# Order changes in a window-attention and ReGLU kernel: heating and bias of unit 1, chain of unit 2, transposes of batch 2, and the end in three pieces

## The chip, the cores and the metric

The kernel runs on one core of one Trainium2 chip. The metric is the device time of one execution in microseconds. Each kernel is timed in several executions, and one execution carries a trace. A page of the profile gives the *span* (first to last instruction); the device time is about 1.7 us longer than the span. The engines are PE (TensorE, the matmuls; PEld is its weight loads), DVE (VectorE), ACT (ScalarE) and POOL (GpSimd); PSUM is the memory in which matmul results land. The *granted clock* is the share of PE's full clock that it was given. Ratios are the mean time of one kernel's fast runs (all within 1.5% of its fastest) over that of the kernel before in the same rounds, so they are not quite the ratios of the medians quoted.

## The reference, cut to what matters

```python
# q, k, v: (8, 8, 576, 64); attention over a causal window of 64 tokens
scores = scale * np.matmul(q, k.transpose(0, 1, 3, 2))
mask = (rel >= 0) & (rel < 64)
attn = softmax(np.where(mask, scores, -1e9))
attn_out = np.matmul(attn, v)
# then a gated feed-forward net on all 4608 tokens of 512 features
x = attn_out.transpose(0, 2, 1, 3).reshape(4608, 512)
out = (np.maximum(x @ w_gate, 0) * (x @ w_val)) @ w_out      # 1536 hidden features
```

## The kernel before

Attention runs in 24 *units* of 192 tokens of one sequence (three units to a batch), the feed-forward net in 12 *tiles* of 384 tokens, two units to a tile. A hand-written scheduler, the weaver, interleaves them: each piece of work is queued with a planned time, and while the feed-forward matmuls are emitted, whatever is due is emitted between them. A planned time fixes only the order of instructions on each engine. Hidden features are made in 12 blocks `f`; a hidden tile of the text is one PSUM tile `h` (gate or value side), and a *gate* is the DVE product `g_sb` of both sides.

One unit needs: scores (`st`, PE), exponentials (`p`, ACT), masks (DVE), values (`pv`, PE), then copies of the values out of PSUM (`xv`, ACT), transposes of the sums (`sT`, DVE), reciprocal, spreading (`rs`) and multiply (`xt`, DVE). Units 0 and 1 use a bias matmul in place of the mask. q and k of each batch pass through DVE transposes first (`qT`, `kT`, about 1.25 us each, four to a batch).

```python
def heat(n, to, start=True):            # matmuls on zeros, to keep PE busy
    for _ in range(n):
        nc.tensor.matmul(to, zero[:, 0:128], zero[:, 0:to.shape[1]], ...)

def plan_unit(u, T, exp=0.8, mask=1.5, pv=3.9, copy=(4.7, 6.0),
              norm=(4.8, 6.1, 7.4, 8.7), gap=0.6):
    W.at(T, lambda: u_st(u))
    for g in range(G):
        W.at(T + exp + gap * g, lambda g=g: u_exp(u, g))
        W.at(T + mask + gap * g, lambda g=g: u_mask(u, g))
    ...                                 # copies at copy, values at pv
    # norm: two halves of the sums' transposes, reciprocal + spreading, multiply

W.at(5.4, lambda: heat(10, units[0]["spare"], False))
W.at(8.7, lambda: u_st(0, (0,)))
W.at(9.5, lambda: heat(8, units[0]["spare"], False))
W.at(11.0, lambda: u_st(0, (1,)))
...                                     # cut: exponentials and copies
W.at(11.4, lambda: u_pv(0, (0, 1)))
W.at(11.45, lambda: u_bias(1, (2, 3)))  # half of unit 1's bias
W.at(11.5, lambda: u_pv(0, (2, 3)))
W.at(11.6, lambda: u_bias(1, (0, 1)))
W.at(11.7, lambda: u_st(1))
...                                     # cut
plan_unit(2, 24.0, *fast)
...
for t in range(3, NU // 2):             # T grows by 26.525 a tile
    for u, at, tr in ((2 * t, T + 0.5, early), (2 * t + 1, T + 13.2, late)):
        if u == 2 * UB:
            plan_batch(2, 36.9, (50.0, T + 0.3, T + 1.7, T + 3.1))
        ...
    plan_unit(2 * t, T + (5.0 if t == 3 else 0.5))
    plan_unit(2 * t + 1, T + 13.2, ...)
```

The softmax here doesn't subtract the row's maximum and nothing guards it: scores larger than these inputs give would overflow.

Of the kernel before, what the change touches and what calls it, by code (L numbers as in the profile page):

```python
# [9 lines left out]
FP32 = mybir.dt.float32  # L10
# [32 lines left out]
def kernel(  # L43
# [10 lines left out]
    nc = tc.nc  # L54
    B, H, S, D = q.shape
    DM = H * D
# [9 lines left out]
    TT = 2 * U  # L66
# [10 lines left out]
    f_sb = ctx.enter_context(tc.tile_pool(name="f_sb", bufs=3))  # L77
# [5 lines left out]
    wo = persist.tile([128, NF, DM], FP16)  # L83
# [44 lines left out]
    W = Weaver()  # L128
    units = {}
# [32 lines left out]
    def qk_load(b, name, hh):  # L162

        tile_ = nat[b, name, hh] = a_in.tile([128, S // 32 * D], FP16, name=f"{name}{hh}", bufs=2)
        src = (q if name == "q" else k)[b, G * hh:G * hh + G]
        nc.gpsimd.dma_start(tile_, src.rearrange("h (i j) d -> (h i) (j d)", i=32))
# [31 lines left out]
    def u_bias(u, gs=range(G)):  # L198

        d = units.setdefault(u, {})  # L200
        if "st" not in d:
            st_tiles(u)
        d["biased"] = True
        for to in d["st"][0] + d["st"][1] if u == 0 else [d["st"][0][g] for g in gs]:
            n = to.shape[1] // 256
            nc.tensor.matmul(to.rearrange("p (h c) -> p h c", h=n), ident,  # L206
                             bias.rearrange("p w c -> p (w c)")[:, None, :].to_broadcast([128, n, 256]),
                             start=True, stop=False, skip_group_check=True)

    def heat(n, to, start=True):  # L210

        for _ in range(n):
            nc.tensor.matmul(to, zero[:, 0:128], zero[:, 0:to.shape[1]], start=start, stop=start, skip_group_check=not start)
# [140 lines left out]
    def plan_batch(b, load, trans):  # L354
        for i, (name, hh) in enumerate((n, hh) for n in "kq" for hh in range(2)):
            if load is not None:
                W.at(load, lambda name=name, hh=hh: qk_load(b, name, hh))
            W.at(trans[i], lambda name=name, hh=hh: qk_trans(b, name, hh))
# [90 lines left out]
    def output_last(t):  # L449

        last = TT // 128 - 1
        output(t, range(last))
        W.drain()
        for col in range(2):
            op = op_tile()
            for f in range(NF):
                g_sb, _ = gs[t]
                nc.tensor.matmul(op[:, 0:256], g_sb[:, f, bass.ds(last * 128, 128)], wo[:, f, 256 * col:256 * col + 256],  # L458
                                 start=(f == 0), stop=(f == NF - 1))
            parts = ((0, 256, nc.scalar.copy, nc.sync),) if col == 0 else (  # L460
                (0, 128, nc.scalar.copy, nc.scalar), (128, 256, nc.vector.tensor_copy, nc.sync))
            o_sb = f_sb.tile([128, DM], FP32, name="o_sb")
            for c0, c1, copy, queue in parts:
                copy(o_sb[:, c0:c1], op[:, c0:c1])
                queue.dma_start(out[bass.ds(t * TT + last * 128, 128), 256 * col + c0:256 * col + c1], o_sb[:, c0:c1])

    def output_by_rows(t):
        ops = [op_tile() for _ in range(TT // 128)]
# [8 lines left out]
    with tc.manual_schedule():  # L477
        for hh in range(2):
            k_first(hh)
        for hh in range(2):  # L480
            qk_load(0, "q", hh)
        warm = consts.tile([128, 2], FP32)
        nc.vector.memset(warm, 0.0)
        nc.scalar.activation(warm[:, 1:2], warm[:, 0:1], ACT.Exp)
        zero = consts.tile([128, 512], FP16)
        nc.vector.memset(zero, 0.0)
        st_tiles(0)
        heat(12, units[0]["st"][1][3])
        bands()
        constants()  # L490
        v_ones(1, nc.vector)
        for hh in range(2):
            for part in range(2):
                k_round(hh, part, 2)
        W.at(5.0, lambda: qk_trans(0, "k", 0, 0, 9))
        W.at(5.1, band_bias)
        W.at(5.2, lambda: qk_trans(0, "k", 0, 9, 18))
        W.at(7.0, lambda: qk_trans(0, "q", 0))
        W.at(8.6, lambda: qk_trans(0, "k", 1, 0, 9))
        W.at(8.7, lambda: qk_trans(0, "k", 1, 9, 18))  # L500
        W.at(9.9, lambda: qk_trans(0, "q", 1))
        G3, V3, O3 = ([(wt, src, f0, f0 + 4) for f0 in (0, 4, 8)]
                      for wt, src in ((wg, moe_w_gate), (wv, moe_w_val), (wo, moe_w_out)))
        W.at(5.5, lambda: v_load(0))
        W.at(5.6, lambda: v_load(1))
        W.at(6.4, lambda: w_load(*G3[0], 13.7))
        W.at(6.5, lambda: w_load(*V3[0], 16.3))
        W.at(6.6, lambda: w_load(*G3[1], 18.9))
        W.at(9.9, lambda: w_load(*V3[1], 21.5))
        W.at(9.9, lambda: w_load(*G3[2], 24.1))  # L510
        W.at(9.9, lambda: w_load(*V3[2], 26.7))
        W.at(12.3, lambda: v_load(2))
        W.at(12.6, lambda: w_load(*O3[0], 31.2))
        W.at(12.7, lambda: w_load(*O3[1], 33.8))
        W.at(12.8, lambda: w_load(*O3[2], 36.4))
        plan_batch(1, None, (37.5, 39.0, 40.4, 41.8))
        W.at(13.0, lambda: qk_load(1, "k", 0))
        W.at(13.0, lambda: qk_load(1, "k", 1))
        W.at(13.0, lambda: qk_load(1, "q", 0))
        W.at(13.0, lambda: qk_load(1, "q", 1))  # L520
        W.at(13.1, lambda: v_load(3))
        W.at(30.0, lambda: v_load(4))
        W.at(30.1, lambda: v_load(5))
        W.at(5.3, lambda: u_bias(0))
        W.at(5.4, lambda: heat(10, units[0]["spare"], False))
        W.at(8.7, lambda: u_st(0, (0,)))
        W.at(9.5, lambda: heat(8, units[0]["spare"], False))
        W.at(11.0, lambda: u_st(0, (1,)))
        for g in range(G):
            W.at(9.6 + 0.05 * g, lambda g=g: u_exp(0, g, 0))  # L530
            W.at(11.1 + 0.05 * g, lambda g=g: u_exp(0, g, 1))
            W.at(12.0 + 0.05 * g, lambda g=g: u_copy(0, g))
            W.at(12.3 + 0.05 * g, lambda g=g: u_exp(1, g))
        W.at(11.4, lambda: u_pv(0, (0, 1)))
        W.at(11.45, lambda: u_bias(1, (2, 3)))
        W.at(11.5, lambda: u_pv(0, (2, 3)))
        W.at(11.6, lambda: u_bias(1, (0, 1)))
        W.at(11.7, lambda: u_st(1))
        W.at(11.9, lambda: u_sum(0, 0))
        W.at(12.0, lambda: v_before(1))  # L540
        W.at(12.1, lambda: u_sum(0, 1))
        W.at(12.2, lambda: u_back(0))
        W.at(12.5, lambda: u_norm(0))
        W.at(12.6, lambda: u_pv(1))
        W.at(12.7, lambda: u_sum(1, 0))
        W.at(12.8, lambda: u_sum(1, 1))
        for n in range(4):
            W.at(12.9, lambda n=n: u_copy(1, n))
        W.at(13.2, lambda: u_back(1))
        W.at(13.3, lambda: u_norm(1))  # L550
        W.at(21.0, lambda: v_ones(2, nc.vector))
        W.at(18.0, lambda: v_before(2))
        W.at(21.0, lambda: v_ones(0, nc.vector))
        W.at(22.0, k_zeros)
        fast = 0.8, 1.5, 3.9, (4.1, 5.3), (4.2, 5.4, 6.4, 7.5), 0.5
        plan_unit(2, 24.0, *fast)
        plan_unit(3, 42.5, *fast)
        plan_unit(4, 50.0)
        plan_unit(5, 58.0, *fast)
        T = 68.4  # L560
        early, late = (-7.4, -6.0, -4.6, -3.2), (-20.3, -18.9, -17.5, -16.1)
        for t in range(3, NU // 2):
            for u, at, tr in ((2 * t, T + 0.5, early), (2 * t + 1, T + 13.2, late)):
                if u == 2 * UB:
                    plan_batch(2, 36.9, (50.0, T + 0.3, T + 1.7, T + 3.1))
                elif u % UB == 0:
                    plan_batch(u // UB, at + tr[0] - 10, [at + x for x in tr])
            plan_unit(2 * t, T + (5.0 if t == 3 else 0.5))
            plan_unit(2 * t + 1, T + 13.2, copy=(4.7, 5.8), norm=(4.8, 5.9, 6.9, 8.0))
            T += 26.525  # L570
        W.advance(13.7)
        ready(1)
        hidden(0, 0, U, 0, 4, 4)
        ready(2)
        hidden(0, U, TT, 0, 4, 4)
        hidden(0, 0, TT, 4, NF, 4)
        output_by_rows(0)
        ready(3)
        hidden(1, 0, U)
        output(1, (0,))  # L580
        ready(4)
        hidden(1, U, TT)
        output(1, (1, 2))
        for t in range(2, NU // 2):
            ready(2 * t + 2)
            hidden(t, 0, TT)
            (output if t < NU // 2 - 1 else output_last)(t)
        W.drain()
# [30 lines left out]
```

## Time and profile before

| | kernel before |
|---|---|
| timed executions | 342.64 to 342.87 us (median 342.76, 3 runs) |
| the traced execution | 344.84 us, span 343.1, mean granted TensorE clock 0.995 |
| busy share PE / DVE / ACT | 97% / 73% / 54% |

Views of the trace are shown in the prediction. In a timeline line, the numbers are start and length in us; the bracket is the engine's idle time before the instruction and what ended it. In a line of windows, the numbers are the window and its length, then busy us of PE, PEld, DVE, ACT, POOL, then granted clock, DMA share and GB/s. The 16 pairs of L305 that the prediction times are a weight load and a 128-column value matmul each.

### The profile page before, as it was taken

Reading aid. Unit: us, or ns where it says so; the run is one execution under the profiler, and the core shown is the slowest. Engines: PE = TensorE matmul, PEld = TensorE weight load, DVE = VectorE, ACT = ScalarE, POOL = GpSimd, SP = SyncE. Lnnn points to the kernel's source line nnn. Section 1 sums busy time; section 2 is a strip of 40 time slices with the busy share of each in tenths; the row PEclk is TensorE's granted clock in tenths of the full one; section 3 lists DMA queues with packets and bytes.
Section 4 is the critical chain, followed back from the end, with each engine's and each line's share of the span. In section 5 each row is a group of like instructions: output and inputs, shape, how many; then the busy total and the mean of one; then the engine's idle time right before and its main releaser. Section 6 shows DMA issues by size and latency. Waiting matters only on the chain.

```text
span 343.1 us, 7364 instructions
## 1 busy us (share of the span) xinstructions
PE 332.7 (97%) x2950; PEld 201.2 (59%) x2950; DVE 251.5 (73%) x452; ACT 186.7 (54%) x383; POOL 65.7 (19%) x99
## 2 busy tenths in 40 slices
PE   8789999999999999999999999999999999999996
PEld 4476477956646556555555655654664664664653
DVE  5587948998898775797888873878968974875430
ACT  4547157645737546556565565564664663763322
POOL 8723421420122211220120410420120200000000
PEclk9899999999999999999999999999999999999999
DMA  8999998790361941961352962874306401001002
GB/s 214 176 206 196 201 167 150 87 178 31 25 84 42 166 58 63 158 74 63 23 48 77 116 80 92 89 100 105 25 5 119 33 2 71 22 2 62 31 2 93
DMA packets 59666, 30.29 MB, mean 88 GB/s; under 512 B 46064, under 2 KB 51056, under 8 KB 59632
## 3 DMA queue, kind: packets, MB, share of 16 engines
q0 software_dynamic: 53872, 19.21, 52.4%
q1 hardware_dynamic: 5616, 10.55, 8.3%
q8 instruction: 23, 0.38, 0.4%
q14 instruction: 11, 0.09, 0.1%
q10 hardware_dynamic: 144, 0.07, 0.1%
HBM read 39.58 MB, written 9.44 MB: 143 GB/s over the span
## 4 chain that ended last, share of the span: by engine, by line
PE 80%; DVE 11%; issue 4%; DMA 2%; POOL 1%; ACT 1%; ACTq 0%; DVEq 0%; POOLq 0%
PE h L412 48%; PE op L426 21%; PE pv L305 6%; DVE sT L335 3%; PE st L246 3%; DVE g_sb L400 2%; DMA v<-in_v_dram 2%; DVE qT L184 2%; DVE xt L350 1%; DVE rs L344 1%; DVE p L266 1%; DVE kT L184 1%; PE op L458 1%; PE pv L287 1%; PE st L206 1%
## 5 line engine op out<-in xcount | busy, mean ns | idle before, releaser
L400 DVE TENSOR_TENSOR g_sb<-r_sb,h 128x384 f16<-128x384 f32 x144 | 78.3, 549 | 54.0 <-PE h L412 45.8
L412 PE MATMUL h<-xt,wg 128*128 128x384 f16 (+1 forms) x640 | 116.5, 310 | 0.7 <-DVE xt L350 0.7
L412 PE MATMUL h<-xt,wv 128*128 128x384 f16 (+1 forms) x640 | 116.6, 310 | 0.2 <-ACT r_sb L397 0.2
L397 ACT ACTIVATE r_sb<-h 128x384 f32<-128x384 f32 x144 | 71.2, 496 | 51.3 <-PE h L412 43.1
L426 PE MATMUL op<-wo,g_sb 128*128 128x512 f16 x420 | 93.3, 379 | 0.5 <-DVE g_sb L400 0.5
L412 PEld LDWEIGHTS <-wg 128*128 128x128 f16 x640 | 59.3, 98 | 34.7 <-DVE xt L350 1.4
L412 PEld LDWEIGHTS <-wv 128*128 128x128 f16 x640 | 59.7, 98 | 32.0 <-issue 0.5
L192 POOL DMA_DIRECT2D v<-in_v_dram x48 | 40.4, 846 | 189.5 <-PE pv L305 170.1
L426 PEld LDWEIGHTS <-g_sb 128*128 128x128 f16 x420 | 40.9, 98 | 48.8 <-issue 1.1
L335 DVE STREAM_TRANSPOSE sT<-pv 64x384 f32<-64x384 f32 x88 | 51.1, 580 | 11.4 <-PE pv L305 9.8
L260 ACT ACTIVATE p<-st 128x512 f16<-128x512 f32 x92 | 49.9, 604 | 11.6 <-PE st L246 11.4
L433 ACT COPY o_sb<-op 128x512 f32<-128x512 f32 x35 | 20.5, 586 | 61.1 <-PE op L426 61.0
L323 ACT COPY xv<-pv 64x384 f32<-64x384 f32 x88 | 41.7, 474 | 18.3 <-DVE sT L335 8.5
L266 DVE TENSOR_TENSOR p<-p,mask 128x512 f16<-128x512 f16 x88 | 34.2, 420 | 6.5 <-ACT p L260 5.9
L305 PE MATMUL pv<-p,v 128*128 128x128 f16 x352 | 24.1, 219 | 0.4 <-DVE p L266 0.4
L344 DVE STREAM_TRANSPOSE rs<-rT 128x768 f32<-128x768 f32 x24 | 23.5, 979 | 0.8
L305 PEld LDWEIGHTS <-v 128*128 128x128 f16 x352 | 21.6, 98 | 3.7 <-issue 0.9
L350 DVE TENSOR_TENSOR xt<-xv,rs 128x768 f16<-128x768 f32 x24 | 22.7, 947 | 0.7
L184 DVE STREAM_TRANSPOSE kT<-k 128x576 f32<-128x576 f32 (+1 forms) x18 | 19.8, 1119 | 1.9 <-ACT k L177 1.8
L184 DVE STREAM_TRANSPOSE qT<-q 128x576 f32<-128x576 f32 x16 | 19.0, 1239 | 0.9 <-DMA q<-in_q_dram 0.8
L246 PE MATMUL st<-qT,kT 32*128 32x128 f16 x768 | 16.1, 215 | 2.2 <-DVE qT L184 2.2
L246 PEld LDWEIGHTS <-kT 32*128 32x128 f16 x768 | 11.5, 92 | 10.5 <-issue 10.5
(46 smaller groups left out, 80.3 us busy)
## 6 DMA issues: line engine op xcount, KB each, us to landing
out_dram<-o_sb SPq DMA_DIRECT2D x35, 256.0 KB, 2.0
v<-in_v_dram POOLq DMA_DIRECT2D x38, 128.0 KB, 4.0
q<-in_q_dram POOLq DMA_DIRECT2D x16, 288.0 KB, 8.3
k<-in_k_dram POOLq DMA_DIRECT2D x14, 288.0 KB, 6.4
wg<-in_moe_w_gate_dram POOLq DMA_DIRECT2D x3, 512.0 KB, 11.2
wv<-in_moe_w_val_dram POOLq DMA_DIRECT2D x3, 512.0 KB, 13.0
wo<-in_moe_w_out_dram POOLq DMA_DIRECT2D x3, 512.0 KB, 16.3
k<-in_k_dram SPq DMA_DIRECT2D x2, 576.0 KB, 4.0
```

Source lines behind the costliest of these rows:

```text
L184: nc.vector.transpose(dst.rearrange("p (i j) -> p j i", i=32)[:, j0:j1], src[:, j0:j1])
L192: nc.gpsimd.dma_start(v16[p0:128, w, :, 0:64], v[b, :, k0 + p0:k0 + 128].rearrange("h p d -> p h d"))
L246: nc.tensor.matmul(d["st"][hh][g][:, c:c + 128], kT[rows, hh, ks + 128 * w:ks + 128 * w + 128, dh], qT[rows, hh, ks + 64 * w:ks + 64 * w + ...
L260: nc.scalar.activation(d["p"][g].rearrange("p h c -> p (h c)"), d["st"][0][g], ACT.Exp, scale=scale)
L266: nc.vector.tensor_tensor(p, p, mask.rearrange("p w c -> p (w c)")[:, None, :].to_broadcast([128, 2, 256]), MUL)
L305: nc.tensor.matmul(d["pv"][c % 2][:, c // 2, e, 64 * w:64 * w + 128], v16[:, w, 128 * h - 64 * e:128 * h - 64 * e + 128], d["p"][h % G][:, ...
L323: nc.scalar.copy(d["xs"][rows, n::2], d["pv"][n][rows, :, e, 0:U])
L335: nc.vector.transpose(to[64 * e:64 * e + 64, half::2], d["pv"][half][64 - 64 * e:128 - 64 * e, :, e, 0:U])
L397: nc.scalar.activation(part(r_sb), part(h1), ACT.Relu)
L400: nc.vector.tensor_tensor(g_sb[:, f:f + w, c0:c1], part(r_sb), part(h2), MUL)
L412: nc.tensor.matmul(h[:, b * n:b * n + n], wt[:, c, (f + b) * 128:(f + b) * 128 + 128], xt[:, c, c0:c1], start=(c == 0), stop=(c == NC - 1))
L426: nc.tensor.matmul(op, g_sb[:, f, bass.ds(sub * 128, 128)], wo[:, f], start=(f == 0), stop=(f == NF - 1))
```

## The change

Four parts. *Start:* more heating, and half of unit 1's bias ahead of unit 0's values, where PE waited. *Unit 2:* its normalising goes behind all gates of tile 0, into tile 0's output matmuls, and batch 1's transposes follow in one block. *Batch 2:* its first transpose leaves unit 4 (planned at 50.0) and joins the other three at the head of tile 2; units 6 and 7 move a little. *End:* the last 128 rows are computed in three column pieces with a PSUM tile each, so that ACT and DVE need not take turns on one (in the trace before, DVE's last copy starts at 340.21 us, once ACT's copy of the same tile, at 339.91 for 0.27 us, has ended).

```diff
-        for col in range(2):
+        o_sb = f_sb.tile([128, DM], FP32, name="o_sb")
+        for c0, c1, copy, queue in ((0, 256, nc.scalar.copy, nc.sync), (256, 384, nc.scalar.copy, nc.scalar),
+                                    (384, 512, nc.vector.tensor_copy, nc.sync)):
             op = op_tile()
...                                                   # cut: matmul, copy and store of each piece
-        plan_batch(1, None, (37.5, 39.0, 40.4, 41.8))
+        plan_batch(1, None, (37.0, 37.8, 39.4, 40.8))
-        W.at(5.4, lambda: heat(10, units[0]["spare"], False))
+        W.at(5.4, lambda: heat(11, units[0]["spare"], False))
-        W.at(9.5, lambda: heat(8, units[0]["spare"], False))
+        W.at(9.5, lambda: heat(11, units[0]["spare"], False))
-        W.at(11.45, lambda: u_bias(1, (2, 3)))
+        W.at(11.35, lambda: u_bias(1, (2, 3)))
-        plan_unit(2, 24.0, *fast)
+        plan_unit(2, 23.0, 0.8, 1.5, 3.9, (4.7, 6.0), (4.8, 7.4, 11.2, 11.3), 0.6)
-                    plan_batch(2, 36.9, (50.0, T + 0.3, T + 1.7, T + 3.1))
+                    plan_batch(2, 36.9, (T - 0.8, T + 0.6, T + 2.4, T + 4.2))
-            plan_unit(2 * t, T + (5.0 if t == 3 else 0.5))
-            plan_unit(2 * t + 1, T + 13.2, copy=...)
+            plan_unit(2 * t, T + (6.0 if t == 3 else 0.5))
+            plan_unit(2 * t + 1, T + (13.6 if t == 3 else 13.2), copy=...)
```

## The prediction

> **What bounds the kernel now.** I read the page's busy table and slices first, then one-microsecond windows over the first 20 us, then the timeline wherever PE has a gap, because a gap of the bounding engine is all that a change of order can win.

> ```profile
> PE 332.7 (97%) x2950; PEld 201.2 (59%) x2950; DVE 251.5 (73%) x452; ACT 186.7 (54%) x383; POOL 65.7 (19%) x99
> ...
> PE   8789999999999999999999999999999999999996
> ```

> PE bounds it: 97% busy, the three slices with less being the first ones, and the last slice the tail. All idle time of PE is 343.1 - 332.7 = 10.4 us, so an ideal reordering could hardly win 3%. But busy is not the same as fast. Windows over the start (columns: window and its length, busy us of PE, PEld, DVE, ACT, POOL, then the granted TensorE clock, DMA share, GB/s):

> ```profile
> 8.73:12.14 3.41, 1.83 (x44) 1.21 (x33) 2.07 (x3) 1.94 (x7) 3.07 (x5) 1.00 2.71 133
> 12.14:15.56 3.42, 3.42 (x34) 1.72 (x34) 1.36 (x4) 1.44 (x5) 2.31 (x3) 0.50 1.25 204
> 15.56:18.97 3.41, 2.17 (x65) 1.68 (x64) 3.23 (x7) 2.38 (x5) 1.27 (x2) 1.00 1.24 206
> ```

> I placed the borders where the one-microsecond windows turn: 0.57 in 12 to 13 us and 0.72 in 15 to 16 us put them at 12.14 and 15.56. For 3.42 us the clock is halved, right after 3.41 us in which PE was busy for only 1.83 us; 2.17 us busy in the stretch after it did not halve it again. The timeline of the start (start, length, engine, what; the wait and its releaser in brackets) shows the path in this stretch:

> ```profile
> 10.97 0.41 PE L246 MATMUL st<-qT,kT 32*128 32x128 f16 x16 [1.06 <-DVE qT L184]
> ...
> 12.08 0.29 PE L287 MATMUL pv<-p,v 128*64 128x128 f16 x2 [0.52 <-DMA v<-in_v_dram]
> ...
> 12.95 1.03 PE L206 MATMUL st<-bias,ident 128*128 128x512 f16 x2
> ...
> 15.75 0.64 PE L246 MATMUL st<-qT,kT 32*128 32x128 f16 x32
> ...
> 16.43 2.06 ACT L260 ACTIVATE p<-st 128x512 f16<-128x512 f32 x4
> ...
> 19.08 1.50 PE L412 MATMUL h<-xt,wg 128*128 128x192 f16 x16
> ```

> PE waits 0.52 us for unit 0's values, which land at about 12.03, and only then, at half clock, does unit 1's bias (1.03 us for two 512-column matmuls). The later gaps, in time order:

> ```profile
> 38.57 1.02 PE L426 MATMUL op<-wo,g_sb 128*128 128x512 f16 x4 [0.22 <-DVE g_sb L400]
> ...
> 39.90 6.20 PE L426 MATMUL op<-wo,g_sb 128*128 128x512 f16 x28 [0.31 <-DVE g_sb L400]
> ...
> 49.46 0.42 PE L246 MATMUL st<-qT,kT 32*128 32x128 f16 x16 [0.37 <-DVE qT L184]
> ...
> 59.63 1.25 DVE L184 STREAM_TRANSPOSE kT<-k 128x576 f32<-128x576 f32 x1
> 60.72 1.40 DVE L266 TENSOR_TENSOR p<-p,mask 128x512 f16<-128x512 f16 x4
> 61.28 1.39 PE L305 MATMUL pv<-p,v 128*128 128x128 f16 x16
> ...
> 93.69 1.46 PE L305 MATMUL pv<-p,v 128*128 128x128 f16 x16
> ...
> 340.21 0.29 DVE L464 COPY o_sb<-op 128x128 f32<-128x128 f32 x1 [7.52 <-ACT o_sb L464]
> ```

> The reader is to see that each is PE held by DVE: output matmuls waiting for gates stuck behind unit 2's normalising, scores waiting for a late transpose, value matmuls that take 1.39 or 1.46 instead of their usual 1.06 because masks are late. At the end, the DVE copy starts only when ACT's copy of the same PSUM tile ends.

> [...]a 3.42 us stretch at 0.50, the two 512-column bias matmuls in it take 1.03 us with the last one's drain, against 0.22 us for one (7.77 us for 36) later. [...]here 16 such pairs (L305) take 0.89 us in the chain, 56 ns each, and I use 56. [...]

> **The change part by part.** The instruction orders of both kernels differ only before hidden tile 3 and at the end. From tile 3 to the last rows, DVE, ACT and PE do the same in the same order, so what is won early is kept.

> *Start.* Heat goes from 10 + 8 to 11 + 11 matmuls of 256 columns. At 0.107 us each, that fills idle time (0.41 us before the first scores, 1.06 us before the second) and delays nothing. Half of unit 1's bias moves ahead of unit 0's value matmuls, into the 0.52 us wait; its PSUM slots came free with exponentials of about 9.6 us. The activity of the window 8.73 to 12.14 rises by 3 x 0.107 + 0.43 to about 2.6 us[...]. I expect no half-clock stretch. Then from 12.08: first half of the values 0.5 (to 12.55); the second half needs the exponentials that end at 12.62, so 12.68 to 13.15; second bias 0.43; scores 0.57, to 14.15 instead of 16.39. But ACT and DVE take turns on unit 0's second pair of PSUM values: copy 0.32, two transposes 0.65, copy 0.32, with handovers, 13.2 to 14.6. So the exponentials start at 14.6 instead of 16.43: 1.8 us won, not 2.2. Unit 0's tokens are ready in time (transposes, 0.30 + 0.98 + 0.96, about 16.6) and the first weights landed at about 15.8, the second at 18.4 for use at 18.6. **-1.8 us.**

> *Unit 2 in tile 0.* From the 384-column matmuls at 24.96 to the output's end at 46.10 are 21.14 us. Without waits the work there is 64 hidden matmuls of 0.1625 (10.4), scores 0.57, values 0.9 and the output's 36 matmuls 7.77: 19.64. So 1.5 us are lost to waits and their drains. The change puts the gates before reciprocal, spreading and multiply (0.30 + 0.98 + 0.94 us on DVE). I laid DVE's new order out: last gates end 0.7, 1.0 and 1.5 us after the output starts, and the three output tiles need slots at 0, 0.86 and 1.7 us. No wait remains. **-1.4 us.** Batch 1's transposes (4 x 1.25) now follow in one block, ended 45.2, since the last q lands at about 43.95, whatever PE does. Unit 3's scores come at about 45.4, so the 0.37 us wait goes, just. **-0.4 us**, and DMA lets little more be won here.

> *Batch 2 in tile 2.* The transpose at 59.63 leaves the path of unit 4's masks: 1.39 becomes 0.9 of issue time: **-0.5 us.** It goes to the start of tile 2. There, from 76.50 (first hidden matmul) to 95.64 (output), 19.14 us pass, and work without waits is 24 x 0.65 + 2 x 0.6 + 2 x 0.9 = 18.6. In the new order the scores of units 6 and 7 come after 10 and 19 hidden tiles instead of 8 and 18, and only 9, not 11, hidden tiles follow unit 6's values. DVE after those values needs transposes and gates 3.75, reciprocal, spread and multiply 2.25, masks and gates 2.25: 8.25 us until the last mask. PE has 7.3 us of work there. Unit 6's values end at 11.35 instead of 10.02 us of the tile, so output starts at 11.35 + 8.75 = 20.1 instead of 19.14. **+1.0 us.** This is the least sure term.

> *End.* PE: 12 x 0.109 + 24 x 0.056 = 2.65 us, against 24 x 0.109 = 2.62. The last copy no longer queues behind ACT's 0.27 us. Its store is as before. **-0.3 us.**

> Sum: -1.8 - 1.4 - 0.4 - 0.5 + 1.0 - 0.3 = -3.4 us, 342.76 to 339.4. I move 0.1 down, since my count for tile 2 lets DVE overlap nothing: **339.3 us**.

> **The rivals.** *The clock stays halved.* [...]only the moved bias is won: 0.9 us instead of 1.8, total 340.2. Against it: 2.6 us busy. [...] *The new bound is DMA.* Values for unit 2 land at about 30.1 us by my reading, needed at 30.2; the last q at 43.95. If these landings move late, 0.5 to 1 us of the start is given back: 340. *DVE in tile 2 does not bind*, because its short instructions overlap at their edges: then tile 2 costs 0 and the total is 338.3. *DVE binds worse*: the block of transposes at the head of tile 2 holds gates back, and every hidden tile has to wait: 340.5.

> **Range and chances.** One term failing costs about 1 us, two of them failing the same way 1.7. 8 in 10: 337.6 to 340.9. Faster by over 2% needs less than 335.9, more than all my gains with no loss (338.4): 0.02. Slower by over 2%: 0.01. Within 2%: 0.97.

> **What would show it.** Right: granted clock 1.00 in every stretch from 12 us on; first hidden matmul at about 17.3 instead of 19.08; output of tile 0 from 35.0 to 42.8 without waits on gates; unit 3's scores in one piece; unit 4's values in 1.06; unit 7's values stretched beyond 1.46, or a gate wait before them; DVE's last copy not released by ACT. Wrong: a stretch at 0.50 anywhere, waits on v or qT from DMA, tile 2 taking under 19.2 us.

## The result, and the profile after

The changed kernel took 340.94 us (median of 4 runs, 340.77 to 341.37) against 342.75 (4 runs): ratio 0.9949, 95% interval 0.9932 to 0.9966. That is 1.8 us faster, where 3.4 were predicted, and just outside the range that ended at 340.9. Yet the traced executions differ by 4.0 us (span 343.1 to 339.1), more than predicted. So the question is not where the changed kernel lost time, but which execution of the kernel before the trace shows.

The busy table and PE's slices of the changed kernel:

```profile
PE 331.3 (98%) x2966; PEld 201.3 (59%) x2966; DVE 252.3 (74%) x452; ACT 186.3 (55%) x383; POOL 65.6 (19%) x99
...
PE   8899999999999999999999999999999999999996
```

The same three windows as before show the clock at 1.00 throughout:

```profile
8.73:12.14 3.41, 3.41 (x65) 2.24 (x65) 2.00 (x4) 2.14 (x8) 3.23 (x6) 1.00 2.37 143
12.14:15.56 3.42, 2.18 (x63) 1.43 (x60) 2.92 (x8) 2.59 (x9) 2.15 (x3) 1.00 1.24 203
15.56:18.97 3.41, 3.14 (x56) 2.92 (x54) 3.30 (x7) 2.52 (x8) 1.50 (x2) 1.00 1.24 207
```

The timeline of the changed kernel, at the places that the prediction marked:

```profile
12.79 0.60 PE L206 MATMUL st<-bias,ident 128*128 128x512 f16 x2
...
14.28 2.07 ACT L260 ACTIVATE p<-st 128x512 f16<-128x512 f32 x4
...
16.94 1.50 PE L412 MATMUL h<-xt,wg 128*128 128x192 f16 x16
...
34.78 7.93 PE L426 MATMUL op<-wo,g_sb 128*128 128x512 f16 x36
...
45.29 0.64 PE L246 MATMUL st<-qT,kT 32*128 32x128 f16 x32
...
57.15 1.06 PE L305 MATMUL pv<-p,v 128*128 128x128 f16 x16
...
86.54 0.64 PE L246 MATMUL st<-qT,kT 32*128 32x128 f16 x30 [0.28 <-DVE sT L335]
...
90.14 0.81 PE L412 MATMUL h<-xt,wv 128*128 128x384 f16 x4 [0.26 <-DVE g_sb L400]
90.79 1.32 PE L305 MATMUL pv<-p,v 128*128 128x128 f16 x16
...
336.19 0.29 DVE L462 COPY o_sb<-op 128x128 f32<-128x128 f32 x1 [7.21 <-PE op L460]
```

Tile 0's output is one unbroken group, unit 3's scores too, unit 4's values take 1.06 instead of 1.39, tile 2 has two new waits, of unit 7's scores on unit 6's transposes of the sums and of a hidden tile on a gate, and the last copy waits for PE and no longer for ACT. Everything in the prediction's list of what would show it right is there, although the total was missed: the list looks at the changed kernel alone and could not show that the trace of the kernel before was an exception. Laid side by side, the starts of the same instructions in both traces give the balance by stage. The third column is from a later trace of the kernel before (run b_look below), in the state of its timed executions:

| stretch (us) | first trace of before to after | b_look to after | predicted |
|---|---|---|---|
| to the first hidden matmul | 19.08 to 16.94: -2.1 | 16.68 to 16.94: +0.3 | -1.8 |
| from there to tile 1's first hidden matmul, lengths | 26.86 to 25.61: -1.25 | 26.86 to 25.61: -1.25 | -1.4 |
| to the hidden matmul after unit 3's scores | -0.6 | -0.55 | -0.4 |
| to tile 2's first hidden matmul (unit 4's values) | -0.5 | -0.5 | -0.5 |
| tile 2, to its output | 19.14 to 19.92: +0.8 | +0.8 | +1.0 |
| the rest, with the end | -0.3 | -0.3 | -0.3 |
| span | -4.0 | -1.6 | -3.4 |

The +0.3 of the first line is no more than executions with one start differ among themselves (16.68 to 17.32 us in the traces at full clock).

### The profile page after: what moved, and what is told of

Its sections match the earlier page's. It is cut to its first block, busy times and chain, and to the rows that moved or that the text cites. A ratio compares the mean times of both kernels' runs of the same rounds, so it can differ in the third digit from the quotient of the medians.

```text
span 339.1 us, 7390 instructions
## 1 busy us (share of the span) xinstructions
PE 331.3 (98%) x2966; PEld 201.3 (59%) x2966; DVE 252.3 (74%) x452; ACT 186.3 (55%) x383; POOL 65.6 (19%) x99
## 4 chain that ended last, share of the span: by engine, by line
PE 85%; DVE 10%; issue 3%; ACT 1%; ACTq 0%
PE h L412 51%; PE op L426 21%; PE pv L305 6%; PE st L246 3%; DVE sT L335 3%; PE st L213 2%; DVE g_sb L400 2%; DVE xt L350 1%; DVE qT L184 1%; DVE rs L344 1%; PE op L460 1%; DVE kT L184 1%; DVE p L266 1%; ACT p L260 1%; PE st L206 1%
## 5 line engine op out<-in xcount | busy, mean ns | idle before, releaser
L412 PE MATMUL h<-xt,wg 128*128 128x384 f16 (+1 forms) x640 | 116.4, 310 | 0.7 <-DVE xt L350 0.7
L412 PE MATMUL h<-xt,wv 128*128 128x384 f16 (+1 forms) x640 | 116.4, 310 | 0.3 <-DVE g_sb L400 0.3
L400 DVE TENSOR_TENSOR g_sb<-r_sb,h 128x384 f16<-128x384 f32 x144 | 78.1, 548 | 49.0 <-PE h L412 47.0
L426 PE MATMUL op<-wo,g_sb 128*128 128x512 f16 x420 | 93.0, 379 | 0.0
L412 PEld LDWEIGHTS <-wg 128*128 128x128 f16 x640 | 59.4, 98 | 34.7 <-DVE xt L350 1.4
L412 PEld LDWEIGHTS <-wv 128*128 128x128 f16 x640 | 59.6, 98 | 32.1 <-issue 0.5
L426 PEld LDWEIGHTS <-g_sb 128*128 128x128 f16 x420 | 40.9, 98 | 47.8 <-DVE g_sb L400 0.4
L335 DVE STREAM_TRANSPOSE sT<-pv 64x384 f32<-64x384 f32 x88 | 51.1, 581 | 11.5 <-PE pv L305 10.1
L260 ACT ACTIVATE p<-st 128x512 f16<-128x512 f32 x92 | 49.9, 604 | 10.2 <-PE st L246 10.1
L266 DVE TENSOR_TENSOR p<-p,mask 128x512 f16<-128x512 f16 x88 | 34.5, 419 | 7.0 <-ACT p L260 6.3
L305 PE MATMUL pv<-p,v 128*128 128x128 f16 x352 | 23.6, 219 | 0.4 <-DVE p L266 0.3
L305 PEld LDWEIGHTS <-v 128*128 128x128 f16 x352 | 21.5, 98 | 3.1 <-issue 0.7
L184 DVE STREAM_TRANSPOSE kT<-k 128x576 f32<-128x576 f32 (+1 forms) x18 | 19.8, 1120 | 3.1 <-ACT k L177 1.8
L184 DVE STREAM_TRANSPOSE qT<-q 128x576 f32<-128x576 f32 x16 | 19.0, 1240 | 1.2 <-DMA q<-in_q_dram 1.1
L246 PE MATMUL st<-qT,kT 32*128 32x128 f16 x768 | 16.1, 215 | 0.7 <-DVE qT L184 0.4
L246 PEld LDWEIGHTS <-kT 32*128 32x128 f16 x768 | 11.4, 92 | 8.7 <-issue 8.1
```

The source lines that it names most:

```text
L184: nc.vector.transpose(dst.rearrange("p (i j) -> p j i", i=32)[:, j0:j1], src[:, j0:j1])
L246: nc.tensor.matmul(d["st"][hh][g][:, c:c + 128], kT[rows, hh, ks + 128 * w:ks + 128 * w + 128, dh], qT[rows, hh, ks + 64 * w:ks + 64 * w + ...
L260: nc.scalar.activation(d["p"][g].rearrange("p h c -> p (h c)"), d["st"][0][g], ACT.Exp, scale=scale)
L266: nc.vector.tensor_tensor(p, p, mask.rearrange("p w c -> p (w c)")[:, None, :].to_broadcast([128, 2, 256]), MUL)
L305: nc.tensor.matmul(d["pv"][c % 2][:, c // 2, e, 64 * w:64 * w + 128], v16[:, w, 128 * h - 64 * e:128 * h - 64 * e + 128], d["p"][h % G][:, ...
L335: nc.vector.transpose(to[64 * e:64 * e + 64, half::2], d["pv"][half][64 - 64 * e:128 - 64 * e, :, e, 0:U])
```

## The experiments

Fifteen runs in four groups. Each group ran on one chip and shares its rounds of the kernel before, whose median there was 342.85 to 343.01 (in the last group it is a single execution; the first and third group, on one chip, have seven executions of it in common).

**Theory A:** the traced execution of the kernel before was not typical. Its half-clock stretch is missing in most executions, so the start part removes something that mostly isn't there. **Theory B:** the stretch is in every execution, and the timed ones are shorter for another reason.

**b_again, the kernel before unchanged.** No edit.

> The kernel before, unchanged, to see its timed executions one by one. Its profiled execution took 344.84 us, its timed ones 342.64 to 342.87. Theory A (the profiled execution was not typical: its half-clock stretch of 3.42 us, which makes the mean granted clock 0.995, is missing in the timed ones): mean clock 0.999 or 1.000 in the timed executions, about 342.75 us, span about 341.0. Theory B (the stretch is in every execution, and profiling itself cost the 2 us): mean clock 0.995 throughout, with times near 342.75.

Timed: 342.53 to 342.93 (4 runs), ratio 0.9995, and the record has the mean clock of each: 1.0, 0.999, 0.999 and 1.0. That is what A expected; B's 0.995 is in none of them. The traced execution came out at 574.95 us, a state apart that no expectation named: granted clock 0.56 from 6.9 us to the last instruction. PE was busy for 567.6 of the 573.2 us of its span, and the clock stayed there; the trace does not show what held it. It says nothing on A or B and was left out of the fast runs.

```profile
PE   9999999999999999999999999999999999999997
...
PEclk7555555555555555555555555555555555555555
```

**start_only, the start part alone on the kernel before.**

```diff
-heat(10, ...)  heat(8, ...)   W.at(11.45, lambda: u_bias(1, (2, 3)))
+heat(11, ...)  heat(11, ...)  W.at(11.35, lambda: u_bias(1, (2, 3)))
```

> The kernel before with the start part alone (heat 11 and 11, half of unit 1's bias ahead of unit 0's values). Theory A: with the clock full in both, only the place of the bias is left to win, 0.3 to 0.6 us: about 342.3. Theory B: the 1.8 us of my prediction or more, about 340.8.

Measured: 342.87 (342.59 to 343.64), ratio 1.0002, interval 0.9989 to 1.0014. Nothing is won: B's 1.8 us is excluded. A's own 0.3 to 0.6 for the place of the bias is not there either; at most 0.4 us lies in the interval.

**no_start, the start part undone in the changed kernel.** The reverse edit.

> The changed kernel with the start part undone. Theory A: 0.3 to 0.6 us slower than the changed kernel, about 341.4. Theory B: 1.8 us slower or more, about 342.8, with mean clock 0.995.

Measured: 341.17 median, ratio 0.9954, against 0.9949 and 0.9941 of the changed kernel in its two groups. Its traced execution happened to have the stretch, clock 0.995, and took 342.79; its five timed ones took 340.6 to 341.4. One kernel, one chip, two states: the stretch belongs to an execution, not to the kernel, and costs some 1.6 us here.

**b_look, the kernel before, traced once more.** No edit.

> The kernel before once more, for a trace of it without the half-clock stretch. If theory A holds, its time is about 342.8 us, its mean clock 1.0 and its first hidden matmul at about 17.3 us (17.32 in the trace with unit 2's part alone, whose start is that of the kernel before), not 19.08. If it falls in the stretch again: 344.8 and clock 0.995.

Measured: 342.46 us, span 340.7, clock 1.0. This settles it. The same windows, in the same kernel as in the prediction:

```profile
8.73:12.14 3.41, 2.74 (x60) 1.75 (x54) 2.52 (x6) 2.27 (x8) 3.41 (x6) 1.00 2.37 141
12.14:15.56 3.42, 2.31 (x67) 1.61 (x67) 2.76 (x6) 2.67 (x9) 2.69 (x4) 1.00 1.24 208
15.56:18.97 3.41, 3.14 (x52) 2.92 (x47) 3.20 (x8) 2.39 (x8) 0.78 (x2) 1.00 1.24 205
```

And its timeline of PE: no wait for the values by DMA, and the bias takes 0.60 instead of 1.03.

```profile
10.99 0.30 PE L287 MATMUL pv<-p,v 128*64 128x128 f16 x4
...
12.66 0.60 PE L206 MATMUL st<-bias,ident 128*128 128x512 f16 x2
13.20 0.64 PE L246 MATMUL st<-qT,kT 32*128 32x128 f16 x32
...
16.68 1.49 PE L412 MATMUL h<-xt,wg 128*128 128x192 f16 x16
```

Its chain of waits (start, length, what) shows why not even the moved bias is worth anything at full clock:

```profile
12.77 0.33 ACT xv L319
...
13.13 0.66 DVE sT L332 x2
...
14.02 2.08 ACT p L260 x4
```

Unit 1's exponentials wait for ACT, which takes turns with DVE on unit 0's PSUM values until 14.0. Scores are through at 13.84, so the second bias has slack. What the move takes from the bias it adds to the values, which feed that chain: the first ones start at 11.66 us in the changed kernel's trace, behind the moved bias, and at 10.99 here. At half clock scores had ended at 16.39, and then the bias was on the path.

**heat_none, the kernel before without its 18 heating matmuls.**

```diff
-W.at(5.4, lambda: heat(10, units[0]["spare"], False))
-W.at(9.5, lambda: heat(8, units[0]["spare"], False))
```

> The kernel before without its 10 and 8 heating matmuls. PE is then idle for most of 6.9 to 11 us[...]. Theory A (timed executions obey the same clock[...]): now every execution has the stretch at half clock, 1.5 to 2.2 us slower than before, about 344.7. Rival C (timed executions keep the full clock whatever PE does): no slower than before, 342.8, or up to 0.2 faster.

Measured: traced 342.43 at clock 1.0; timed 344.13, 343.94, 342.86, 344.23, 343.82, so about 1 us over the kernel before in most. The ratio from fast runs is 1.0017, interval 0.9996 to 1.0038. Neither C nor "every execution" holds: some have it and some not. The record has the mean clock of the timed ones: 0.995 in the four slow ones, 0.999 in the one of 342.86. Two more traces were taken to see the stretch itself:

> The kernel before without its 18 heating matmuls, one more trace. Its timed executions were 342.86 to 344.23 us, four of five over 343.8, while its traced one took 342.43 at full clock. If the slow ones have a half-clock stretch (theory A), a trace of 343.8 us or more shows a mean clock near 0.995 and a stretch of some 3.4 us; a trace near 342.5 shows none. Rival: the slow ones lose their time elsewhere, and a trace of 343.8 us or more has clock 1.0.

> The same once more, since one trace can fall on either side: clock near 0.995 with over 343.8 us, or clock 1.0 with about 342.5.

Measured: 344.88 and 345.11 us, both at mean clock 0.99. The windows of the first of them:

```profile
9.00:13.00 4.00, 2.25 (x42) 1.42 (x34) 2.55 (x5) 2.65 (x9) 3.92 (x6) 0.64 2.22 152
13.00:17.00 4.00, 3.49 (x52) 1.86 (x51) 2.32 (x6) 1.44 (x4) 1.95 (x3) 0.50 1.24 205
17.00:21.00 4.00, 3.29 (x54) 2.96 (x54) 3.25 (x7) 3.11 (x10) 1.00 (x2) 1.00 1.24 207
```

The slow traces have the stretch, and here it is twice as long, from 10.1 to 17.0 us; the four slow timed executions, at 0.995, fit one of 3.4 us. Since the record has the mean clock of nearly every execution, they can be counted. Leaving out the two slow ones (574.95 and 350.69 us), a mean clock of 0.995 or less, so by estimate a stretch somewhere (3.41 us at half clock lower the mean over 343 us by 0.005), is found in 6 of 8 executions without heating, in 4 of 53 with the old start and heating, and in 2 of 29 with the new start (343.64 us in start_only and 342.64 in norm_late2, both at 0.994). So the stretch was rarer with heating; that the new start makes it rarer than the old one is not shown.

> The changed kernel with the start of the kernel before, one more trace. The first took 342.79 us at clock 0.995, its five timed ones 340.6 to 341.4. Theory A: most executions have no stretch, so about 341.1 us at clock 1.0; with the stretch again 342.8 and 0.995.

Measured: 341.55 us, clock 1.0: the kernel that had the stretch in its first trace hasn't it in the second.

**unit2_only, unit 2's plan and batch 1's transposes alone.**

```diff
-plan_batch(1, None, (37.5, 39.0, 40.4, 41.8))     plan_unit(2, 24.0, *fast)
+plan_batch(1, None, (37.0, 37.8, 39.4, 40.8))     plan_unit(2, 23.0, ..., (4.8, 7.4, 11.2, 11.3), 0.6)
```

> The kernel before with unit 2's plan and batch 1's transposes alone. The traces of both kernels give 1.24 us for tile 0 and 0.56 for unit 3's scores, so 1.8 us: 341.0, the whole measured gain. If DMA's landing of the last q had held unit 3's scores in executions with an earlier start, only 1.2 us: 341.6.

Measured: 341.15 median (340.8 to 343.03), ratio 0.9954, interval 0.9930 to 0.9979. As expected: this part alone makes practically the whole gain (its execution of 343.03 us had the stretch, clock 0.995), and the last q's landing did not hold it up.

**tile2_only, batch 2 and units 6 and 7 alone.**

```diff
-plan_batch(2, 36.9, (50.0, T + 0.3, T + 1.7, T + 3.1))    T + 5.0   T + 13.2
+plan_batch(2, 36.9, (T - 0.8, T + 0.6, T + 2.4, T + 4.2)) T + 6.0   T + 13.6
```

> The kernel before with batch 2's transposes and units 6 and 7 moved, alone. 0.5 us won at unit 4's values, 0.8 lost in tile 2: 0.3 slower, about 343.1. If tile 2's loss exists only after unit 2's part, 0.5 faster: 342.3.

Measured: 343.26 (342.84 to 343.57), ratio 1.0011, interval 0.9997 to 1.0025: 0.4 us slower in the ratio, in line with 0.3, though the interval reaches zero. The trace has the same waits as the changed kernel, of which this is the second:

```profile
92.18 0.81 PE L412 MATMUL h<-xt,wv 128*128 128x384 f16 x4 [0.26 <-DVE g_sb L400]
92.83 1.32 PE L305 MATMUL pv<-p,v 128*128 128x128 f16 x16
```

**no_tile2, that part undone in the changed kernel.** The reverse edit.

> The changed kernel with batch 2's transposes and units 6 and 7 as before. Comparing the two traces, unit 4's values gain 0.5 us by the change and tile 2 loses 0.8: undoing both should be 0.2 to 0.4 us faster than the changed kernel, about 340.6. If DVE in tile 2 does not bind in typical executions, undoing it costs 0.5: 341.4.

Measured: 340.72, ratio 0.9938, interval 0.9926 to 0.9950. Its difference from the changed kernel is in the expected direction and below what these intervals separate.

**a_again, the changed kernel as the base of the second group.** No edit.

> The changed kernel, unchanged, as the base of this group. About 340.95 us, ratio to before 0.995. If the state of the clock at the start is drawn anew in each execution, its trace may show another border for the first half-clock stretch than 7.2 us, and times up to 341.4.

Measured: 340.98, ratio 0.9941, interval 0.9924 to 0.9958. Its matmuls in the first trace had been at the slow rate until 7.3 us; here until 4.8. (The clock column reads 1.00 in these first microseconds, before the trace's first record of the clock; the slow rate is read from the 512-column heating matmuls, which start 0.43 us apart until then and 0.21 afterwards.) The time at which the slow rate ends does change between executions, as expected; in the prediction's trace it is 5.3 us.

**end_only, the three-piece end alone.** The diff's first hunk.

> The kernel before with the three-piece end alone. By the two traces the end gained 0.3 us: 342.5. If the narrow last matmuls cost PE as much as the copy saves, nothing: 342.8.

Measured: 342.48, ratio 0.9990, interval 0.9977 to 1.0003: consistent with 0.3 us, not separated from nothing. In the trace the DVE copy (at 337.58) waits for PE, 7.20 us, and no longer for ACT.

**norm_late2 and norm_late3, attempts at a better tile 2.** Unit 6's tokens are not needed before tile 3, so its last three DVE steps can go behind unit 7's masks, which hold PE.

```diff
-plan_unit(2 * t, T + 6.0)
+plan_unit(2 * t, T + 6.0, norm=(4.8, 6.1, 11.05, 11.1))      # for tile 2 alone
 # batch 3's transposes, offsets: before  (-20.3, -18.9, -17.5, -16.1)
 # norm_late2:                            (-16.8, -15.4, -8.0, -5.5)
 # norm_late3:                            (-20.3, -18.05, -17.5, -16.1)
```

> The changed kernel with unit 6's reciprocal, spreading and multiply moved behind unit 7's masks, and batch 3's transposes behind unit 7's tokens. If tile 2 is bound by the DVE chain in front of unit 7's masks, as the trace shows (0.78 us lost there against before), this takes back 0.8 to 1.3 us: 339.7 to 340.1. If DVE's total work in tile 2 is the bound, nothing: 340.9.

Measured: 342.64, ratio 0.9982: a miss. Its traced execution was slow (clock 0.95 from 5.9 us on, 350.69 us), so only the order of events can be read from it: unit 7's values take 1.07, but in tile 3 the moved q transposes hold PE up, 1.1 us by two waits, of which this is one:

```profile
110.26 0.82 PE L412 MATMUL h<-xt,wv 128*128 128x384 f16 x4 [0.32 <-ACT r_sb L397]
```

> The changed kernel with unit 6's reciprocal, spreading and multiply behind unit 7's masks, as in the run before, but of batch 3's transposes only the second k moved, behind unit 7's tokens. The earlier attempt lost its gain in tile 3, where its q transposes held gates and ReLUs up (1.1 us of waits). Now tile 2 should win 0.8 to 1.1 and tile 3 lose nothing: 339.8 to 340.2, ratio 0.991. If the tokens of unit 7 become late for tile 3, the gain is eaten: 340.9.

Measured: 340.58 (340.4 to 341.08), ratio 0.9935, interval 0.9922 to 0.9948. Tile 2 now takes 71.96 to 91.21 = 19.25 us instead of 19.92:

```profile
90.31 1.06 PE L305 MATMUL pv<-p,v 128*128 128x128 f16 x16
...
91.21 7.93 PE L426 MATMUL op<-wo,g_sb 128*128 128x512 f16 x36
```

Half of that comes back in tile 3, where unit 8's values break into two groups. It has the lowest median of all, but its interval overlaps that of the changed kernel, so it is not shown to be better.

## Why the prediction was wrong, point by point

**The start, -1.8 us: wrong, and it alone makes the miss.** Measured alone, it is 1.0002. In the prediction's words the step was that from 12.14 to 15.56 "the clock is halved", and that removing this stretch and the 0.52 us wait for the values wins 1.8 us. As a reading of that one trace it held (19.08 to 16.94). But it was taken as a property of the kernel. The traced execution took 344.84 us, the timed ones 342.76, and the sum was subtracted from the latter. The stretch comes in some executions and not in others, as no_start, b_look and the clocks of the timed executions show, and the timed median is one without it. At full clock the old start reaches its first hidden matmul at 16.68 to 17.32 us and the new one at 16.87 to 17.25. That the changed kernel's trace has no stretch, as predicted, is therefore no success of the heating: most executions with either start have none (49 of 53 with the old one, 27 of 29 with the new one). Nor was it shown that 2.6 us of busy PE would avert it: that was the estimate from 1.83 and 2.17 us in one trace. Nor did the heating "delay nothing" in that trace: unit 0's first scores, whose transpose ended at 8.49 us, start behind it at 9.09. The second scores (10.78) still follow their transpose (10.72), so it cost nothing there. The remaining five terms sum to -1.6 us, which from 342.76 gives 341.16; measured were 340.94 and 340.98.

**Unit 2 in tile 0, -1.4, and unit 3's scores, -0.4: right.** 1.25 and 0.55 in the traces, and 1.8 by the medians of unit2_only (1.6 by its ratio, which includes the execution with the stretch). "Just" in time was right as well: qT ends as the scores begin.

**Batch 2: right in both signs.** -0.5 at unit 4's values, +0.8 for +1.0 in tile 2, at the place named: from the end of unit 6's values to the end of unit 7's last mask the chain of waits runs through DVE, for 8.0 us (83.54 to 91.57) where 8.25 were counted. The two waits of PE, at unit 7's scores and on a gate, lie within that chain. tile2_only: +0.4.

**The end, -0.3: right in the trace,** not separable in the timed runs.

**The rivals.** None was right. "The clock stays halved" would have left 340.2, and it looked on the wrong side: the clock was not halved in the first place. The 2.6 us of busy PE held against it were no proof either: in the traces busy time alone does not decide (see Open). The range had no case in which the kernel before is already without the stretch, although the 2.1 us between its traced and its timed executions pointed there.

```profile
6.26:9.67 3.41, 1.62 (x25) 1.10 (x24) 2.64 (x5) 1.47 (x5) 3.41 (x6) 1.00 1.68 171
```

There the clock stayed full after 1.62 us, and PE was nearly idle from 7.5 to 10.6 us in this execution. So the record starts at different times (5.32, 6.73 and here 6.26 us), and low busy time goes with the drop, but it does not decide alone. Why v landed later in the prediction's trace was not tested; no_start's trace has the stretch without a wait for v.

## What to carry to other kernels

Compare the traced execution's own time with the timed median before using any duration of it: here 2.1 us of difference were the very 2 us that seemed to be there to win. Where the record lists the clock of each timed execution, read it before taking more traces. A gain that rests on a transient state (here the half clock, in 4 of 53 executions with the old start and heating, and the 0.52 us wait for v, which b_look does not have) needs a second trace; a gain that rests on the order of one engine's instructions was predicted here to 0.2 us from a single one. When work moves out of one stage, lay out the engine that receives it: in tile 2 the wait on DVE's chain cost 0.8 us, 0.3 us more than the move had won.
